# Fourteen unread products on TensorE during a weight load, and a further search of the order of work

## The chip, the cores and the metric

The kernel runs on one core of a Trainium2 chip. The metric is the time of one execution in microseconds of device time. Differences rest on several rounds, and I give them as ratios with a 95% interval. The record marks all runs told here as fast, with mean granted clocks of 0.987 to 0.995. The experiments were made on four chips, and the kernel before has a median of 1844.03 us on one and 1851.88 us on another, as far apart as the effects told here; so a ratio is always to before of the same rounds.

## The reference, cut to what matters

Four blocks one after the other, on 2048 tokens of width 512: a memory block A, a linear attention block B, A again, B again. B is short. A is a recurrence: 64 segments of 32 tokens, each attending to 8 memory rows that the segment before it wrote.

```python
for s in range(n_seg):                       # 64 segments of 32 tokens
    h = concatenate([mem, xs])               # 8 memory rows + 32 tokens
    q, k, v = h @ Wq, h @ Wk, h @ Wv         # 32 heads of 128
    p = softmax(mask(q @ k.T * scale))
    o = (p @ v) @ Wo
    mem = o[:8]                              # the next segment waits for this
    outs.append(o[8:])
```

## The kernel before

The kernel is built by a scheduler on the host. Every piece of work is a node with an engine, a cost and what it reads and writes; `schedule` plays them on a model of the engines, and the order that comes out is the fixed program of each engine. The rank of a node is its step times a period plus an offset from a table, and that table is what was searched.

```python
nd.prio = -(step * PERIOD + OFFSET[name][k])          # rank of a node
...
late.append(add("act", lambda a, W=W, v=v: a.dma_start(W[:, :, :], v), 0.5,
                writes=[nm], dsem="d" + nm, lat=t))   # Wq 13.2, Wk 23.7, Wv 34.8 us in the model
```

A projection is 16 products of 512 columns, four column tiles side by side. It is copied out of PSUM, the memory that TensorE's products are written to in this kernel (`pb` in the views), and turned (transposed), for half of the heads by a transposing DMA that the SP engine's queue issues, for the others by TensorE.

```python
QDMA = (True, False)                 # b = 0: by DMA, b = 1: by TensorE
def turned(W, key, blk, bkeys, b, dst, dkey, urgent, dma):
    tl = project(W, key, blk, bkeys, b, urgent)
    nd = evac(img[:, k, :], lambda: tl.f32()[:, :], 512, ...)
    if dma:
        add("sp", lambda e: e.dma_start_transpose(dst..., img[:, k, :]), 1.25, ..., lat=TURN)
        return nd
    ...                              # 16 transposes on TensorE and one copy
```

In the profile PE stands for TensorE's products, PEld for its weight loads, DVE for VectorE, ACT for ScalarE, POOL for GpSimd and SP for SyncE, which issues DMAs; a q after the name is the engine's sequencer, and "<-" names what ended a wait. The lines of the profile: L777 is the projection's product, L799 TensorE's turn, L790 the transposing DMA, L987 the output projection, L861 the memory scores, L1012 the next memory (the last product of a segment's recurrence), L608 and L609 the copies. In the changed kernel they are L789, L811, L802, L999, L873, L1024, L609 and L610, and L737 is the new product.

The softmax here doesn't subtract the row's maximum and nothing guards it: scores larger than these inputs give would overflow.

Of the kernel before, what the change touches and what calls it, by code (L numbers as in the profile page):

```python
# [16 lines left out]
HOP = 0.06  # L17
PE_SWITCH = 0.1
TURN = 1.8
MODE_SLACK = 12.41  # L20

LOOK = 0.074

PERIOD = 13.5
OFFSET = {
    "ld0": (3.45,),
    "ld1": (4.20,),
    "ld2": (-0.95,),
    "ld3": (-2.85,),
    "ld4": (0.40,),  # L30
    "startF": (12.05,),
    "prepF": (-11.05, 4.70, -9.25, -18.05, -7.00, -0.35, -15.95, -12.35, -15.40, 1.00, -1.65),
    "left0F": (-15.70, 1.30, -14.50, 0.25, -0.65, -12.60, 1.65, 6.55),
    "left1F": (15.35, 7.60, -6.60, 4.95, -3.45, 3.20, -0.65, 3.10),
    "leftv0F": (-1.70, -10.10),
    "leftv1F": (9.60, 0.00),
    "leftsF": (3.55, 9.85, 9.35, 1.25),
    "xlF": (1.05,),
    "qk0F": (0.15, 4.00, 2.75, -11.15, 1.55, 1.85, 11.40, 4.05),
    "qk1F": (0.00, -3.50, -2.10, -1.25, -25.90, -0.00, -5.45, 1.95),  # L40
    "v0F": (10.40, 1.50),
    "v1F": (31.95, 7.50),
    "mem0F": (2.55, 0.25, 5.85, -8.30, -1.20, -6.05, 2.15, 3.05, -1.60),
    "mem1F": (17.30, 12.60, 0.00, 1.10, -1.45, -6.00, -2.05, -21.65, 0.45),
    "outF": (1.85, -6.05, -5.85, -2.60),
    "nextF": (-0.45, -5.40, 13.70),
    "xF": (8.05, 1.50, -5.55, 5.05, -0.25, 9.95, 19.65, 5.95, -2.30, 7.20, 8.70, -12.05, -8.75, 4.00, -1.15,
        37.05, 0.30, 2.95, 10.30, 7.45, -2.10, 1.40, 0.10),
    "qk0": (-14.10, 1.50, -0.25, -5.35, -0.10, -0.05),
    "qk1": (1.55, 4.60, -0.05, -0.60, 1.80, 0.00, 7.10, -0.45),  # L50
    "v0": (0.35, -0.20),
    "v1": (5.15, 3.10),
    "mem0": (-5.20, -2.15, -1.60, -49.45, -13.55, -22.95, -3.35, -7.90, 4.70),
    "mem1": (7.10, -4.05, 3.25, -3.75, -2.90, 12.50, 5.15, -16.25, -12.15),
    "out": (-0.75, 4.95, 2.15, 0.00),
    "next": (1.75, 2.45, -4.05),
    "res": (48.90, 6.30, 2.30, -15.10, -1.45, -7.60, -2.50),
    "x": (2.45, 5.90, -2.85, -0.45, 6.20, 0.00, 15.70, -4.55, -22.30, 6.10, -15.10, 5.80, -2.55, 10.75, 6.10,
        0.60, 3.80, 21.60, 10.55, 5.20, 22.60, 29.30, 0.00),
    "prep": (7.35, -10.90, 1.30, 0.30, 10.40, -17.80, -4.90, 5.95, -3.00, -10.50, 9.70),  # L60
    "left0": (-4.00, -0.25, 18.45, -8.00, 1.40, -0.65),
    "left1": (0.10, 3.65, 0.45, 20.95, 3.05, -3.60),
    "leftv0": (32.60, 0.10),
    "leftv1": (11.30, 2.45),
    "lefts": (-2.95, 4.00, 0.50, -7.85),
    "xl": (6.35,),
    "bi": (0.25, -5.75, -1.85, -4.15, 6.60, -10.30, 9.70, -1.75, -6.35, 0.00, -15.35, 2.10, 7.40, -0.60, 21.85,
        -3.30, -3.50, 3.75, 0.00, 7.95, 2.05, 2.85, 12.85),
    "qk0L": (-9.45, 1.80, -2.10, 2.25, -3.65, 4.55, -0.30, 0.30),
    "qk1L": (-2.85, -6.75, -3.35, 4.40, -6.30, 2.10, -0.10, -1.70),  # L70
    "xL": (-6.30, -9.90, -7.95, -2.90, -3.60, 0.00, 4.70, 0.70, -2.85, 14.90, -19.10, 0.15, -0.20, 1.10, 6.60,
        0.15, -2.50, -0.30, -0.90, 0.00, -4.35),
    "lr": (-0.80, 7.55, 8.15, -13.30, 0.15, 7.95),
    "outL": (15.55, 3.95, 0.40, 10.10),
    "resL": (1.40, 4.60),
    "biL": (4.55, -5.70, -1.45, -34.70, -5.20, 0.75, 5.85, -1.90, -1.35, 0.15, 2.50, -24.50, -0.65, -21.55,
        1.05, 0.00, 0.00, 5.40, -1.60, -1.10, 11.15, -3.20, 3.85),
    "bm": (-3.95, -5.05, 16.55, 0.70, -0.20, 3.70, -9.00, 16.45, 0.15, -8.55, 2.25, 4.05, 2.75),
    "boF": (0.00, 7.10, -11.80, 3.35, 0.85, 0.75, -24.50, -13.85),
    "bo": (-1.10, 6.15, -2.70, -2.90, 0.00, -11.50, 1.10, -9.70),  # L80
    "ldL": (22.20, 1.70),
    "boL": (-26.60, 4.05, -1.85, -7.50, -5.65, -6.10, -13.50),
    "boZ": (18.15, -34.85, -14.20, 0.00, 8.30, -5.35, -7.10),
}


# [12 lines left out]
def c_pe(n_mm, n):  # L99
    return n_mm * max(0.0255, (n / 2.4 + 3.0) * 1e-3)  # L100
# [24 lines left out]
class _Prog:  # L125
# [80 lines left out]
    def schedule(self):  # L206
# [92 lines left out]
        def pick_for(e):  # L299
# [7 lines left out]
            while ready[e]:  # L307
# [17 lines left out]
                if pick is None:  # L325
# [3 lines left out]
                    held = item  # L329
                elif nd.prio < pick.prio - MODE_SLACK:  # L330
                    kept.append(item)
# [159 lines left out]
def _build_kernel(nc, A_x, A_mem0, A_Wq, A_Wk, A_Wv, A_Wo, A_seg_len, B_wqkv, B_wo, out):  # L491
# [26 lines left out]
    def sb(name, shape, dt=BF16):  # L518
        return E(nc.sbuf_tensor(name, shape, dt))

    Wq_sb = sb("Wq_sb", [128, 4, H * DH])
# [4 lines left out]
    x_sb = sb("x_sb", [128, NX, D])  # L526
    id_sb = sb("id_sb", [128, 128])
# [74 lines left out]
    P = _Prog(nc, banks)  # L602
    add = P.add
# [13 lines left out]
    x_view = A_x[0].rearrange("(t p) d -> t p d", p=128)  # L617
# [2 lines left out]
    o_view = out[0].rearrange("(t p) d -> t p d", p=128)  # L620
    qk_view = [W.rearrange("(c p) h e -> p c (h e)", p=128) for W in (A_Wq, A_Wk, A_Wv)]

    def x_move(o, i, k, reads, writes, kind, eng="pool"):
        add(eng, lambda e: e.dma_start(o, i), 1.1 if eng == "pool" else 0.4, reads=reads, writes=writes,
            dsem="%s%d" % (kind, k), lat=2.0)

    shift = [0]

    def slot(t):

        return (t + shift[0]) % NX
# [1 line left out]
    P.at(-9000, "ld0")  # L633
    add("sp", lambda s: s.dma_start(mem0_sb[0:M, :], A_mem0[0]), 0.1, writes=[MEM0], dsem="dmem", lat=2.0)
    P.at(-8000, "ld1")
    add("sp", lambda s: s.dma_start(x_sb[:, 0, :], x_view[0]), 0.4, writes=[("x", 0)], dsem="dx0", lat=2.0)
    late = []
    for i, (W, v, nm, t) in enumerate(((Wq_sb, qk_view[0], "Wq", 13.2), (Wk_sb, qk_view[1], "Wk", 23.7),
                                       (Wv_sb, qk_view[2], "Wv", 34.8))):
# [4 lines left out]
    for i in range(4):  # L644
        hs = slice(8 * i, 8 * i + 8)
        add("sp", lambda s, hs=hs: s.dma_start(Wo_sb[:, hs, :], wo_view[:, hs, :]), 0.9, writes=[("Wo", i)],
                 dsem="dWo%d" % i, after=[late[1 + i // 2]], lat=(12.5, 14.5, 7.3, 9.8)[i])
    add("sp", lambda s: s.dma_start(wqkv_sb[:, :, :], B_wqkv.rearrange("(c p) f -> p c f", p=128)), 0.5,
        writes=["wqkv"], dsem="dwqkv", after=[P.nodes[-1]], lat=5.0)
# [38 lines left out]
    for j in range(4):  # L688
        q = slice(32 * j, 32 * j + 32)
        d = j % 2  # L690
# [3 lines left out]
        o = 16 + 224 * d + 96  # L694
        sel(scr_sb[q, o:o + 24], ALU.not_equal, 1.0, -8, [[-1, 24]], 1, *SCR)

        o = 720 + 128 * d
# [3 lines left out]
        for g4 in range(4):  # L701
            o = 464 + 128 * d + 32 * g4 + 24
# [3 lines left out]
        writes=["selx"])  # L706
    add("dve", lambda v: v.tensor_copy(sell_sb[:, :, :].rearrange("p d c -> p (d c)"), scr_sb[:, 464:720]), 0.4, reads=SCR,
        writes=["sell"])
    add("dve", lambda v: v.tensor_copy(selz_sb[:, :, :].rearrange("p d c -> p (d c)"), scr_sb[:, 720:976]), 0.4, reads=SCR,
        writes=["selx"])  # L710
# [4 lines left out]
    tl = P.tile()  # L715
    add("pe", lambda t, tl=tl: t.matmul(tl.f32()[:, 0:128], A8_sb[0:8, :], A8_sb[0:8, :], start=True, stop=True), 0.06,
        reads=XV, tiles=[tl])
    evac(maskbd_sb[:, :], lambda tl=tl: tl.f32()[:, 0:128], 128, tiles=[tl], writes=["maskbd"])
    tl = P.tile()

    def _m0(t, tl=tl):
        for c in range(4):
# [2 lines left out]
    add("pe", _m0, 0.2, reads=[MEM0, "id"], tiles=[tl])  # L725
    evac(memT0_sb[:, :, :], lambda tl=tl: tl.bf16()[:, 0:4 * M].rearrange("p (c m) -> p c m", m=M), 32, tiles=[tl],
         writes=["memT0"])


    ln_no = [0]  # L730
# [31 lines left out]
    def a_layer(base, first):  # L762
        def at(s, name):

            P.at(base + s, name + ("F" if s <= 0 else "L" if s >= NSEG or (s == NSEG - 1 and name in LATE) else ""))
# [233 lines left out]
        def out_block(s):  # L999
            at(s, "out")  # L1000
            keys = [[("oTm", s % NO, b), ("oTx", s % NO, b)] for b in range(2)]
            return out_proj(oTb[:, s % NO, :, :], keys, True)
# [49 lines left out]
        if first:  # L1052
# [7 lines left out]
                writes=[(k, r, b) for k in ("oTx", "oTm") for r in range(NO) for b in range(2)])  # L1060
            add("dve", lambda v: v.memset(Pbx[:, :, :, :].rearrange("p h j q -> p (h j q)").bitcast(F32), 0.0), 0.8,
                writes=[("Pbx", j) for j in range(4)])

        def tokens(t, s):

            if not first:
                b_out(base + s, t, 0)
            elif t:
                at(s, "xl")
                x_move(x_sb[:, slot(t), :], x_view[t], slot(t), [], [("x", slot(t))], "dxl")  # L1070

        at(-4, "start")
        evac(hT[:, 0, 0, :, 0:8], memT0_sb[:, :, :], 32, reads=["memT0"], writes=[("hTm", 0, 0)])
# [3 lines left out]
        for s in range(NSEG):  # L1077
            G, g = divmod(s, 4)
            r2 = s % 2
            blk = hT[:, G % 2, g, :, :]  # L1080
            bk = [("hTm", G % 2, g), ("hTx", G % 2, g)]
            if g == 0 and G + 1 < NT:
                tokens(G + 1, s)
            for b in range(2):
                at(s, "qk%d" % b)
                hs = slice(4 * b, 4 * b + 4)
                turned(Wq_sb, "Wq", blk, bk, b, qT[:, r2, hs, :, :], ("qT", r2, b), True, QDMA[b] and 0 < s < NSEG - 1)
                turned(Wk_sb, "Wk", blk, bk, b, kT[:, r2, hs, :, :], ("kT", r2, b), True, KDMA[b] and 0 < s < NSEG - 1)
            for b in range(2):
                at(s, "v%d" % b)  # L1090
                tl = project(Wv_sb, "Wv", blk, bk, b, True)
                evac(vimg[:, r2, 512 * b:512 * b + 512], lambda tl=tl: tl.f32()[:, :], 512, tiles=[tl],
                     writes=[("v", r2, b)], urgent=True)
            if s + 1 < NSEG:
                for b in range(2):
                    mem_attention(s, b)
            w_of[s] = out_block(s)
            if s + 1 < NSEG:
                next_mem(s, w_of[s])
            if s > 0:  # L1100
                residual((s - 1) // 4, (s - 1) % 4, w_of[s])
                if g == 0:
                    b_in(base + s + 2, G - 1, not first)
            x_attention(s)
            if g == 2 and G + 1 < NT:
                prepare(G + 1, s)
            if s == NSEG - 1:
                at(s, "lr")
                add("pool", lambda p: p.memset(oTl[:, :, 24:32], 0.0), 0.5, writes=[("oTl", b) for b in range(2)])
                left_rows(NT - 1)  # L1110
# [206 lines left out]
```

## Time and profile before

| | before |
|---|---|
| median of the first three runs | 1848.17 us (1845.84 to 1848.36) |
| profiled execution | span 1843.1 us, mean granted clock 0.989 |
| TensorE busy | 1758.4 us, 95% |
| start, up to the end of segment 0's recurrence | 53.8 us |
| segments 3 to 62 of the first A block | 789.3 us |
| segments 63 to 125 of the second A block | 846.8 us |

The last three rows are from the trace: the start of the sixteenth and last L1012 product of each segment. I count segments from 0 to 62 in the first block and from 63 to 125 in the second (the last segment of a block hands no memory on and has no such product). (Some expectations below count ordinally: their tenth segment is 9.) The prediction below shows the page and views of this profile. One more line of the page is needed later, the queue (packets, MB, share of 16 engines' time) that brings instructions:

```profile
q8 instruction: 365, 5.98, 1.3%
```

TensorE's own instructions would explain it: 46,693 products and as many weight loads, 93,386 instructions, over 365 packets are 256 a packet, and 5.98 MB over 365 are 16.4 KB a packet. I call 256 such instructions, or their packet, a block.

### The profile page before, as it was taken

What the parts mean: (1) busy time and instruction counts of PE and PEld (TensorE: products, weight loads), DVE (VectorE), ACT (ScalarE), POOL (GpSimd) and SP (SyncE); (2) the same over time, 40 slices, a digit from 0 to 9 for tenths busy, and PEclk for the clock granted to TensorE, in tenths of its full rate; (3) what the DMA queues carried; (4) which work ended last, traced back from release to release, by engine and by line L of the source; (5) the groups of instructions that cost most, each with busy time, mean ns of one, the idle gap of its engine ahead of it and who ended that gap; (6) DMA issues with size and microseconds to landing.
All of it is one profiled execution on the core that took longest, in us unless ns stands there. A gap on an engine that the chain in (4) does not pass through costs nothing.

```text
span 1843.1 us, 100858 instructions
## 1 busy us (share of the span) xinstructions
PE 1758.4 (95%) x46693; PEld 1194.1 (65%) x46693; DVE 1017.6 (55%) x3168; ACT 1207.6 (66%) x3127; POOL 76.9 (4%) x182
## 2 busy tenths in 40 slices
PE   5899999999999999999799999999999999999997
PEld 2566676666666767666566666666666666666663
DVE  2355555555555555555545555566555556555566
ACT  3566666766666666666466667666667666666665
POOL 3000000000000000000000000000000000000000
PEclk8999999999999999999899999999999999999999
DMA  9312122212221221211012122122122222122223
GB/s 366 85 37 42 38 44 35 47 38 44 38 41 41 35 46 38 44 37 38 22 29 39 37 41 46 39 42 43 38 41 46 41 43 41 41 43 41 52 62 99
DMA packets 218934, 94.85 MB, mean 51 GB/s; under 512 B 202536, under 2 KB 212656, under 8 KB 216976
## 3 DMA queue, kind: packets, MB, share of 16 engines
q1 hardware_dynamic: 211312, 60.22, 17.7%
q0 software_dynamic: 5616, 15.60, 2.9%
q10 hardware_dynamic: 1584, 12.58, 1.7%
q8 instruction: 365, 5.98, 1.3%
q14 instruction: 57, 0.47, 0.1%
HBM read 29.63 MB, written 10.49 MB: 22 GB/s over the span
## 4 chain that ended last, share of the span: by engine, by line
PE 83%; DMA 11%; ACT 3%; DVE 2%; issue 1%; ACTq 0%; DVEq 0%
PE pb L777 38%; PE pb L987 16%; DMA arena_sb<-arena_sb 9%; PE pb L959 3%; PE pb L861 3%; PE pb L1029 3%; PE pb L799 3%; PE pb L1137 3%; PE pb L916 2%; ACT arena_sb L608 2%; PE pb L878 2%; PE pb L1173 1%; DMA Wk_sb<-in_A_Wk_dram 1%; PE pb L892 1%; PE pb L891 1%
## 5 line engine op out<-in xcount | busy, mean ns | idle before, releaser
L608 ACT ACTIVATE arena_sb<-pb 128x512 bf16<-128x512 f32 (+6 forms) x1412 | 727.2, 523 | 359.8 <-PE pb L777 302.1
L777 PE MATMUL pb<-Wq_sb,arena_sb 128*32 128x512 bf16 x5120 | 357.5, 383 | 0.6 <-DMA Wq_sb<-in_A_Wq_dram 0.6
L777 PE MATMUL pb<-Wv_sb,arena_sb 128*32 128x512 bf16 x5120 | 356.9, 382 | 0.1
L777 PE MATMUL pb<-Wk_sb,arena_sb 128*32 128x512 bf16 x5120 | 343.5, 381 | 6.6 <-DMA Wk_sb<-in_A_Wk_dram 5.2
L987 PE MATMUL pb<-Wo_sb,arena_sb 128*32 128x256 bf16 x10368 | 326.4, 273 | 5.8 <-issue 3.7
L987 PEld LDWEIGHTS pb<-Wo_sb,arena_sb 128*32 128x32 bf16 x10368 | 261.5, 96 | 34.8 <-DVE arena_sb L895 13.8
L944 DVE TENSOR_TENSOR arena_sb<-arena_sb 32x256 bf16<-32x256 bf16 x512 | 213.3, 417 | 119.8 <-ACT arena_sb L940 108.7
L609 DVE CAST arena_sb<-pb 128x128 bf16<-128x128 f32 (+3 forms) x334 | 118.5, 355 | 252.5 <-PE pb L1012 201.4
L609 DVE COPY arena_sb<-pb 128x512 bf16<-128x512 bf16 (+2 forms) x352 | 137.7, 392 | 204.5 <-PE pb L799 198.9
L777 PEld LDWEIGHTS pb<-Wk_sb,arena_sb 128*32 128x32 bf16 x5120 | 141.8, 97 | 126.1 <-DMA Wk_sb<-in_A_Wk_dram 5.3
L777 PEld LDWEIGHTS pb<-Wq_sb,arena_sb 128*32 128x32 bf16 x5120 | 133.4, 97 | 113.6 <-DVE arena_sb L609 24.2
L777 PEld LDWEIGHTS pb<-Wv_sb,arena_sb 128*32 128x32 bf16 x5120 | 134.4, 98 | 86.3 <-issue 4.4
L608 ACT ACTIVATE outW_sb<-pb 128x128 fp32r<-128x128 f32 x261 | 72.3, 277 | 114.4 <-PE pb L987 77.1
L799 PEld LDWEIGHTS pb<-id_sb,arena_sb 128*32 128x32 bf16 x4352 | 77.5, 97 | 90.8 <-ACT arena_sb L608 58.1
L959 PE MATMUL pb<-arena_sb 128*128 128x128 bf16 x1024 | 130.9, 217 | 0.0
L799 PE MATMUL pb<-id_sb,arena_sb 128*32 128x128 bf16 x4352 | 109.6, 221 | 14.7 <-ACT arena_sb L608 14.6
L946 DVE TENSOR_TENSOR arena_sb<-arena_sb 32x64 bf16<-32x64 bf16 x512 | 111.1, 217 | 15.8
L960 PE MATMUL pb<-arena_sb 128*128 128x32 bf16 x1024 | 118.3, 177 | 0.0
L868 ACT ACTIVATE arena_sb<-pb 128x256 bf16<-128x256 f32 x252 | 96.1, 383 | 27.3 <-PE pb L861 20.6
L861 PE MATMUL pb<-arena_sb 128*128 128x32 bf16 x2016 | 97.0, 178 | 5.2 <-DMA arena_sb<-arena_sb 4.9
L895 DVE TENSOR_TENSOR arena_sb<-pb,arena_sb 128x128 bf16<-128x128 f32 x252 | 72.2, 286 | 42.0 <-ACT arena_sb L883 27.6
L861 PEld LDWEIGHTS pb<-arena_sb 128*128 128x128 bf16 x2016 | 74.6, 96 | 30.0 <-DMA arena_sb<-arena_sb 6.4
(121 smaller groups left out, 2304.5 us busy)
## 6 DMA issues: line engine op xcount, KB each, us to landing
arena_sb<-arena_sb SPq DMA_TRANSPOSE x368, 2.5
Wq_sb<-in_A_Wq_dram ACTq DMA_DIRECT2D x1, 4096.0 KB, 13.6
Wk_sb<-in_A_Wk_dram ACTq DMA_DIRECT2D x1, 4096.0 KB, 24.3
Wv_sb<-in_A_Wv_dram ACTq DMA_DIRECT2D x1, 4096.0 KB, 34.6
Wo_sb<-in_A_Wo_dram SPq DMA_DIRECT2D x4, 1024.0 KB, 11.6
xs_scratch<-x_sb POOLq DMA_DIRECT2D x32, 128.0 KB, 2.1
pq_scratch<-arena_sb POOLq DMA_DIRECT2D x32, 128.0 KB, 2.8
x_sb<-xs_scratch POOLq DMA_DIRECT2D x16, 128.0 KB, 2.3
```

Of the source, the lines that this page charges most:

```text
L608: return e.activation(o() if callable(o) else o, i() if callable(i) else i, ACTF.Copy)
L609: return e.tensor_copy(o() if callable(o) else o, i() if callable(i) else i)
L777: r = pe.matmul(tl.f32()[32 * j:32 * j + 32, 0:512], blk[:, c, :], W[:, c, o:o + 512], start=(c == 0), stop=(c == 3), tile_position=(0, 32 ...
L799: r = pe.transpose(tt.bf16()[32 * j:32 * j + 32, 128 * i:128 * i + 128], img[:, k, o:o + 32], id_sb[:, :], tile_position=(0, 32 * j))
L861: r = pe.matmul(tl.f32()[:, o:o + 32], kk[:, hh, :, :].rearrange("p j x -> p (j x)"), qT[:, r2, hh, :, 0:8], start=True, stop=True)
L868: add("act", lambda a: a.activation(Pm[:, k, :, :].rearrange("p a q -> p (a q)"), tl.f32()[:, 0:256], ACTF.Exp, scale=SCALE), c_act(256), ...
L895: add("dve", lambda v: v.tensor_tensor(oTb[:, s % NO, 16 * b:16 * b + 16, 0:8], pv.f32()[:, 0:128].rearrange("p (n q) -> p n q", q=8), Rm[ ...
L944: add("dve", lambda v, q=q, j=j: v.tensor_tensor(Pbx[q, :, j, 0:32], Px[q, :, :], Rx[q, :, :], ALU.mult), c_dve(256) + 0.075, reads=["Px", ...
L946: add("dve", lambda v, q=q, j=j: v.tensor_tensor(Pbx[q, :, j, 32:40], PLL[q, g2, :, gl], Rx[q, :, 0:8], ALU.mult), c_dve(64) + 0.075, read ...
L959: pe.matmul(o, vimg[:, r2, e], Pbx[:, hh, :, 0:32], start=True, stop=False)
L960: return pe.matmul(o[:, :, 0:8], vleft[:, g2, e], Pbx[:, hh, :, 32:40], start=False, stop=True)
L987: r = pe.matmul(tl.f32()[32 * j:32 * j + 32, 0:256], oT[:, 4 * hh + n, :], Wo_sb[:, 8 * n + hh, 256 * d:256 * d + 256], start=(hh == 0 and ...
```

## The change

Two intents. TensorE runs fourteen products into a bank that nobody reads, meant, as I take it, to keep its clock at 1.00 where before has it at 0.70 (38 to 39 us) and 0.50 (39 to 45 us). And the table of offsets is searched further, after two token loads were given their real latency in the model. The diff, cut to its core:

```diff
-MODE_SLACK = 12.41
+MODE_SLACK = 11.85
 OFFSET = {
-    "ld0": (3.45,),
+    "ld0": (13.20,),
     ... nearly every other offset changes as well ...
+    "warm": (2000.00,),
 }
...
-    add("sp", ... x_view[0]), 0.4, writes=[("x", 0)], dsem="dx0", lat=2.0)
+    add("sp", ... x_view[0]), 0.4, writes=[("x", 0)], dsem="dx0", lat=8.5)
...
+    def warm(step, n, after):
+        P.at(step, "warm")
+        tl = P.tile()
+        for i in range(n):
+            if i:
+                P.again()
+            add("pe", lambda pe: pe.matmul(tl.f32()[0:32, 0:512], id_sb[:, 0:32], Wq_sb[:, 0, 0:512],
+                                           start=True, stop=True, tile_position=(0, 0)),
+                c_pe(1, 512), reads=["id", "Wq"], tiles=[tl], mode="col", after=after if i == 0 else ())
...
+            if first and s == 0:
+                warm(0, 14, [n for n in P.nodes if n.key == (0, "mem1F", 1)])
```

The token load of the second group gets the same 8.5 us.

## The prediction

> **What bounds the kernel now.** I read the page first: engine shares, then the slices with the granted clock, then the chain that ended last.
>
> ```profile
> PE 1758.4 (95%) x46693; PEld 1194.1 (65%) x46693; DVE 1017.6 (55%) x3168; ACT 1207.6 (66%) x3127; POOL 76.9 (4%) x182
> ...
> PE   5899999999999999999799999999999999999997
> ...
> PEclk8999999999999999999899999999999999999999
> ...
> PE 83%; DMA 11%; ACT 3%; DVE 2%; issue 1%; ACTq 0%; DVEq 0%
> ```
>
> TensorE is busy for 1758.4 of 1843.1 us, so only 84.7 us of the span show it idle, and 83% of the chain is TensorE's own work. Three places are weak: the first two slices (46 us each), the slice in the middle, where one layer ends and the next starts, and the last one. Second view: engine busy time in chosen stretches. The columns are the stretch, its length, the busy time of PE, PEld, DVE, ACT and POOL with instruction counts, the granted clock, the DMA share and GB/s.
>
> ```profile
> 25.60:31.60 6.00, 5.99 (x84) 2.76 (x88) 0.42 (x1) 1.39 (x3) 0.00 (x0) 0.50 1.03 425
> 36.70:39.50 2.80, 0.96 (x41) 0.58 (x45) 0.99 (x4) 1.06 (x4) 0.00 (x0) 0.80 1.10 348
> 39.50:45.10 5.60, 5.60 (x60) 2.07 (x52) 2.94 (x10) 2.18 (x5) 0.00 (x0) 0.50 1.19 264
> 59.90:63.00 3.10, 0.05 (x4) 0.06 (x8) 0.00 (x0) 0.70 (x2) 0.78 (x1) 0.88 0.99 139
> 75.00:870.00 795.00, 777.78 (x21345) 539.12 (x21341) 438.55 (x1393) 541.14 (x1441) 24.39 (x45) 1.00 0.21 40
> 923.00:1771.00 848.00, 831.13 (x22426) 568.42 (x22418) 484.88 (x1537) 572.56 (x1466) 31.11 (x57) 1.00 0.22 41
> ```
>
> The two long rows are the recurrent segments of the two layers: idle 795.00 - 777.78 = 17.2 us and 848.00 - 831.13 = 16.9 us, all at clock 1.00. The other rows are the start. TensorE works at clock 0.50 for about 6 us after the key weights land, and for 5.6 us again with the value weights[...]. Third view: TensorE's timeline there, which says what the idle time was.
>
> ```profile
> 36.67 0.29 PE L916 MATMUL pb<-arena_sb 128*32 128x32 bf16 x18
> 38.19 0.27 PE L916 MATMUL pb<-arena_sb 128*32 128x32 bf16 x14 [1.23 <-issue]
> 38.39 0.28 PE L716 MATMUL pb<-arena_sb 8*128 8x128 bf16 x1
> 39.28 0.41 PE L935 MATMUL pb<-arena_sb,bo_sb 128*32 128x256 bf16 x4 [0.61 <-DVE arena_sb L922]
> 39.48 0.27 PE L932 MATMUL pb<-arena_sb,bo_sb 128*32 128x64 bf16 x4
> 39.55 5.32 PE L777 MATMUL pb<-Wv_sb,arena_sb 128*32 128x512 bf16 x48
> ```
>
> The value products (L777 with Wv) were queued behind the first segment's token scores (L916) and their sums (L935), and the score group was itself cut in two by 1.23 us in which no releaser shows. The list of DMA issues says when the value weights came:
>
> ```profile
> Wv_sb<-in_A_Wv_dram ACTq DMA_DIRECT2D x1, 4096.0 KB, 34.6
> ```
>
> Its issue starts at 1.83 us in the timeline, so they had landed at 1.83 + 34.6 = 36.4 us. The 3.1 us from there to 39.55 is therefore not a wait for that transfer; this is the first thing the change's title leads a reader to misjudge.
>
> [...] clock 0.50 after the pauses before the key weights (5.15 us) and before 62.95 us (3.05 us). Between them, from 36.96 to 39.28, the short groups at 38.19 and 38.39 did not save it: the one-microsecond rows have it at 0.70 from 38 to 39 and at 0.50 after that. [...] Here four column tiles run side by side: 48 value products are 12 rounds, the chain gives them 5.12 us cold, 427 ns a round; 88 warm ones (22 rounds) in the steady state take 4.76 us, 216 ns a round. [...] The page of before has an instruction queue with 365 packets and 5.98 MB, 16.4 KB each[...]. That the 1.23 us cut inside one run of equal products was a late block, at a time when the DMA share is 1.1, is my reading; the trace shows only that no semaphore ended it.
>
> **The change, part by part.**
>
> (a) It adds fourteen products of 512 columns into a spare PSUM bank. They use only the first column tile, so they don't run four abreast: 14 x 216 ns = 3.02 us if warm, 14 x 427 = 5.98 us if cold. Nothing evacuates them, but their tile holds a bank until the next owner takes it. They are ordered after the second memory-score block of the first segment (its L861 products, last group near 36 us in the kernel before) and have the lowest rank of all work, so the host-side scheduler puts them where its own model finds TensorE with nothing else ready. That model knows no cold clock: it loses no time on the 6 us at half speed from 25.6, so it believes TensorE is some 3 us ahead of where it is, with a gap of about 3 us before 36.4. On the chip that gap doesn't stand before 36.4, but after it.
>
> (b) What they buy. If they run from about 36.3, warm (the clock row is 1.00 from 31.7 to 38.3), they end near 39.3: they take the place of the 2.8 us in which TensorE did 0.96 us of work, and the value products start about where they did, 39.3 to 40.3. What changes is their speed: 12 rounds at 216 instead of 427 ns save 12 x 0.211 = 2.53 us; the sums and key products of the rest of the cold stretch (up to 45.15) save about 0.3 more. Gain 2.8 us, less up to 0.8 us for scores and sums that may now come after the fourteen: 2.0 to 2.8. I take 2.5.
>
> (c) Does it reach the end? After 45 us TensorE works without a gap to 59.9, then waits 3.05 us on ACT, which waits on transposes by DMA behind the load of the other block's weights (1536 KB, issued at 53.19 from a queue in order). Earlier evacuations let that queue come to this load earlier, so the wait moves along with the work; the output weights are there at 47.5, when the DMA share drops, and are first used at 51.1, so 2.5 us earlier still finds them. I carry 80%: 2.0 us.
>
> (d) The token loads' model latency goes from 2.0 to 8.5 us for the first two. The measured one is 8.5 us, so the order of the first 15 us now fits the chip, but TensorE waits there for the query weights (14.4 us) anyway: 0 us by itself.
>
> (e) The search: nearly every offset changes, and the slack for staying in a tile mode from 12.41 to 11.85. No arithmetic is added or removed; the same 46,693 products run, plus fourteen. What can be won is bounded by idle time: 34.1 us in the two steady stretches, of which these rows are the largest:
>
> ```profile
> PE pb L799 <- ACT arena_sb L608: 5.3, 10, 1.0
> PE pb L861 <- DMA arena_sb<-arena_sb: 3.9, 6, 1.1
> PE pb L827 <- DMA arena_sb<-arena_sb: 3.2, 5, 0.8
> ...
> PE pb L827 <- DMA arena_sb<-arena_sb: 8.4, 10, 1.4
> PE pb L799 <- ACT arena_sb L608: 4.4, 9, 1.0
> ```
>
> They are the waits of the first layer, then of the second: 25.2 us of stalls under 1.5 us each, the kind that an order removes. Besides, switches between column tiles and whole-array products hide in busy time: the timeline of one segment shows steps of about 0.1 us (406.95 to 407.28, where 0.22 is used), several in each of 128 segments, so 40 to 60 us by estimate, though an already searched order keeps most. I give the search a tenth of 34 + 50 = 84, which is 8 us in its own model, and about 70% of that on the chip: 5.5 us. This is a judgement, not a reading.
>
> (f) Middle (900 to 920: 10.55 us busy of 20) and end (1795 to 1843) are chains of dependent single steps, DVE and ACT in turn; an order shortens them little. One cut of 1.81 us and one of 1.91 us with no releaser stand in the end, at 1797.69 and 1804.45, and may move or stay: +-1 us, mean -1.
>
> Sum: -2.0 + 0 - 5.5 - 1.0 = -8.5 us, from 1848.2 to about 1839.5 us.
>
> **The rivals.** First: the fourteen cost what they buy. If TensorE reaches them late, or they run cold, they delay value weights that have been there since 36.4 us by 3 to 6 us and the gain of (b) is cancelled[...]. For it: the landing at 36.4. Against: the idle time stood there anyway, and the author kept the change. This makes the start 0 to +3 us and the total 1842 to 1845. Second: the gain is made at 40 us and lost at 60, because the wait for the transposes keeps its absolute time with the transfers it stands behind. For it: the DMA share is about 1.0 from 57 to 60. Against: that load starts when its queue gets there, not at a fixed time. Total about 1842. Third: the search finds much more than a tenth, 15 us or more, if it removes the transposes' waits (16.5 of the 25.2 us) and switches as well. For it: nearly all offsets moved. Against: the kernel is already searched, and its busy tenths are all 9. Total about 1830. Fourth: the search fits its model, not the chip; the steady part is unchanged or 3 us worse, total 1846 to 1850.
>
> **Range and chances.** The three runs of before spread over 2.5 us, so noise is about +-1.5 us. Mean 1839.5; the start can give 0 to -4 and the search +2 to -15, which adds up to a range of 1828 to 1847. Faster by over 2% means below 1811.2 us, 37 us off, more than all the steady idle time: 2%. Slower by over 2% means above 1885, which only a broken order could do: 1%. Within 2%: 97%.
>
> **What would show each step.** (a), (b): a row of fourteen products reading Wq into a bank in TensorE's timeline near 36 to 40 us, 216 ns apart, the one-microsecond clock rows at 1.00 through 38 to 46 instead of 0.50, and the value products at 216 ns a round. (c): the pause now at 59.9 to 63.0 comes 2 us or more earlier and is no longer. (e): the idle time of the two steady stretches below 34 us, and the distance from the first segment's value products to the last segment's, in each layer, shorter. If instead the clock is still 0.50 after the fourteen, (b) is wrong; if the steady stretches lose 10 us or more, I have sized the search too small; if they gain, it fits its model alone.

## The result, and the profile after

Ratios here are the mean time of one kernel's fast runs over that of the other's of the same rounds, so they are not quite the ratio of the medians that stand beside them.

| | before | changed |
|---|---|---|
| median of 4 runs | 1847.01 us (1845.42 to 1848.36) | 1845.42 us (1844.32 to 1849.27) |
| ratio | 1 | 0.9995, 95% interval 0.9977 to 1.0014 |
| profiled execution | 1843.1 us | 1847.5 us, the slowest of its four |

The time lies in the range, but the forecast change of 8.5 us is not there. The page of the changed kernel, busy shares, granted clock and chain:

```profile
PE 1758.5 (95%) x46707; PEld 1174.2 (64%) x46707; DVE 1027.4 (56%) x3172; ACT 1205.9 (65%) x3123; POOL 76.9 (4%) x182
...
PEclk9999999999999999999899999999999999999998
...
PE 82%; DMA 12%; ACT 2%; DVE 2%; issue 1%; ACTq 0%; DVEq 0%
```

The first digit of the clock row went from 8 to 9: the start is warmer. And the DMA share of the chain went up from 11 to 12%. The stretches of the prediction, in the changed kernel:

```profile
36.70:39.50 2.80, 1.20 (x21) 0.60 (x22) 1.44 (x6) 0.38 (x1) 0.00 (x0) 1.00 1.09 349
39.50:45.10 5.60, 5.60 (x78) 2.33 (x80) 3.11 (x10) 3.11 (x8) 0.00 (x0) 1.00 1.18 269
59.90:63.00 3.10, 2.31 (x58) 1.42 (x56) 1.12 (x5) 1.53 (x5) 0.00 (x0) 1.00 0.31 111
75.00:870.00 795.00, 772.71 (x21163) 524.35 (x21160) 436.63 (x1381) 537.62 (x1429) 24.38 (x45) 1.00 0.21 40
923.00:1771.00 848.00, 829.25 (x22355) 555.83 (x22348) 489.91 (x1531) 568.30 (x1457) 31.11 (x57) 1.00 0.22 41
```

The clock is 1.00 where it was 0.50 (39.5 to 45.1) and the pause at 60 us is nearly gone. The two long rows show more idle time than before, 41.0 us together against 34.1. Their counts are 182 and 71 products short of before's: the trace has all 46,707 products, but the work stands shifted against these windows (124 more products before 75 us, 92 more after 1771 us). So I use the distances between segments instead. The new products in TensorE's timeline:

```profile
36.15 0.38 PE L737 MATMUL pb<-Wq_sb,id_sb 128*32 128x512 bf16 x1
36.16 0.49 PE L928 MATMUL pb<-arena_sb 128*32 128x32 bf16 x17
38.30 0.27 PE L928 MATMUL pb<-arena_sb 128*32 128x32 bf16 x15 [1.65 <-issue]
38.40 1.67 PE L737 MATMUL pb<-Wq_sb,id_sb 128*32 128x512 bf16 x7
...
40.16 0.39 PE L737 MATMUL pb<-Wq_sb,id_sb 128*32 128x512 bf16 x1
...
40.52 0.81 PE L737 MATMUL pb<-Wq_sb,id_sb 128*32 128x512 bf16 x3
40.96 0.40 PE L789 MATMUL pb<-Wv_sb,arena_sb 128*32 128x512 bf16 x3
41.17 0.38 PE L737 MATMUL pb<-Wq_sb,id_sb 128*32 128x512 bf16 x1
```

They are warm (seven in 1.67 us), but only one runs before the cut, which is now 1.65 us, and the value products start at 40.96 instead of 39.55 us. The pause at 60 us, with the issue of the weight load before it (first before, then the changed kernel):

```profile
53.19 1.52 SPq L648 DMA_DIRECT2D arena_sb<-in_B_wqkv_dram  x1
62.95 0.62 PE L799 MATMUL pb<-id_sb,arena_sb 128*32 128x128 bf16 x16 [3.05 <-ACT arena_sb L608]
```

```profile
48.98 0.58 SPq L649 DMA_DIRECT2D arena_sb<-in_B_wqkv_dram  x1
60.74 0.27 PE L873 MATMUL pb<-arena_sb 128*128 128x32 bf16 x4 [0.80 <-DMA arena_sb<-arena_sb]
```

SP reaches the 1536 KB load after one transpose instead of two, 4.2 us earlier, and the transposes behind it come earlier too. So the changed kernel is ahead: segment 3 ends at 90.54 us instead of 94.87, a lead of 4.3 us. By segment 16 the lead is gone (267.19 against 267.14), at segment 62 the changed kernel is 2.0 us behind, at segment 125 3.9 us. Up to segment 16 the lead is lost in single segments: 5 (0.8 us), 15 (1.7) and 16 (1.0); what segment 8 gains (1.1) segment 9 gives back (1.2), and all others are within 0.3 us. Of the 121 segments from 5 on, 63 take the same time in both kernels to 0.15 us.

### The profile page after: what moved, and what is told of

The parts are those of the page before. It is cut to its first block, busy times and chain, and to the rows that moved or that the text cites. A ratio compares the mean times of both kernels' runs of the same rounds, so it can differ in the third digit from the quotient of the medians.

```text
span 1847.5 us, 100872 instructions
## 1 busy us (share of the span) xinstructions
PE 1758.5 (95%) x46707; PEld 1174.2 (64%) x46707; DVE 1027.4 (56%) x3172; ACT 1205.9 (65%) x3123; POOL 76.9 (4%) x182
## 4 chain that ended last, share of the span: by engine, by line
PE 82%; DMA 12%; ACT 2%; DVE 2%; issue 1%; ACTq 0%; DVEq 0%
PE pb L789 37%; PE pb L999 16%; DMA arena_sb<-arena_sb 11%; PE pb L873 3%; PE pb L971 3%; PE pb L1151 3%; PE pb L1041 3%; PE pb L811 3%; PE pb L928 2%; ACT arena_sb L609 2%; PE pb L890 2%; PE pb L1187 1%; DMA Wk_sb<-in_A_Wk_dram 1%; PE pb L904 1%; PE pb L903 1%
## 5 line engine op out<-in xcount | busy, mean ns | idle before, releaser
L609 ACT ACTIVATE arena_sb<-pb 128x512 bf16<-128x512 f32 (+4 forms) x1410 | 721.2, 519 | 332.8 <-PE pb L789 271.4
L789 PE MATMUL pb<-Wv_sb,arena_sb 128*32 128x512 bf16 x5120 | 352.9, 380 | 0.4 <-issue 0.2
L789 PE MATMUL pb<-Wq_sb,arena_sb 128*32 128x512 bf16 x5120 | 349.0, 383 | 0.9 <-DMA Wq_sb<-in_A_Wq_dram 0.6
L999 PEld LDWEIGHTS pb<-Wo_sb,arena_sb 128*32 128x32 bf16 x10368 | 255.5, 96 | 25.8 <-issue 7.9
L610 DVE COPY arena_sb<-pb 128x512 bf16<-128x512 bf16 (+1 forms) x334 | 134.1, 402 | 204.8 <-PE pb L811 196.7
L610 DVE CAST arena_sb<-pb 128x384 bf16<-128x384 f32 (+3 forms) x354 | 129.9, 368 | 210.1 <-PE pb L1024 157.5
L789 PEld LDWEIGHTS pb<-Wk_sb,arena_sb 128*32 128x32 bf16 x5120 | 135.7, 97 | 132.9 <-DMA Wk_sb<-in_A_Wk_dram 5.7
L789 PEld LDWEIGHTS pb<-Wq_sb,arena_sb 128*32 128x32 bf16 x5120 | 125.4, 97 | 125.9 <-DVE arena_sb L610 24.4
L789 PEld LDWEIGHTS pb<-Wv_sb,arena_sb 128*32 128x32 bf16 x5120 | 127.5, 97 | 89.6 <-issue 2.7
```

The source lines that it names most:

```text
L609: return e.activation(o() if callable(o) else o, i() if callable(i) else i, ACTF.Copy)
L610: return e.tensor_copy(o() if callable(o) else o, i() if callable(i) else i)
L789: r = pe.matmul(tl.f32()[32 * j:32 * j + 32, 0:512], blk[:, c, :], W[:, c, o:o + 512], start=(c == 0), stop=(c == 3), tile_position=(0, 32 ...
L999: r = pe.matmul(tl.f32()[32 * j:32 * j + 32, 0:256], oT[:, 4 * hh + n, :], Wo_sb[:, 8 * n + hh, 256 * d:256 * d + 256], start=(hh == 0 and ...
```

## The experiments

Fifteen runs, each timed in five rounds. All gave correct results.

### Which part of the change does what

Theory 1 said that the start is gained and kept and the new order costs; theory 2, that the lead is given back whatever the order; theory 3, that the order gains and the products cost. Four kernels on one chip. The first is before with the products alone:

```diff
+    def warm(...)        # as in the change
+            if first and s == 0:
+                warm(0, 14, ...)
```

> The kernel before with the fourteen products alone, old order (TensorE's order differs from before's in the first hundred or so groups alone). Theory 1, the start is gained and kept, the searched order costs: 3.0 to 4.5 us under before, and the fourth segment's memory products 3.5 to 4.5 us earlier than the 94.9 us of before. Theory 2, the head start is given back in later waits whatever the order: earlier by 3.5 to 4.5 us at the fourth segment too, but within 1 us of before at the end. Theory 3, the order gains and the products cost: slower than before by 1 us or more.

The second is the changed kernel without them:

```diff
-                warm(0, 14, [n for n in P.nodes if n.key == (0, "mem1F", 1)])
```

> The changed kernel without the fourteen products, new order. Theory 1: 2 to 4 us over before. Theory 2: within 1 us of before. Theory 3: 2 to 5 us under before.

The third takes before's start, no products, and the new offsets of all other segments:

```diff
 OFFSET = {
     ... names that end in F, and ld0 to ld4, as before ...
-    ... all others as before ...
+    ... all others as changed ...
```

> Old offsets for the first segments of each layer and no fourteen products, new offsets for all the rest (TensorE's order is that of before up to group 791, of the changed kernel in the second layer's body). Theory 1: 2 to 4 us over before, all of it after the fifth segment. Theory 2: within 1 us of before. Theory 3: 2 to 5 us under.

The fourth is the changed kernel again, without an edit:

> The changed kernel once more, for five rounds and a second trace. All theories: within 0.15% of before, as its first four runs had it (0.9995). If a second trace loses its time in other segments than the first (there: the tenth, sixteenth and seventeenth, forty-fourth), single late segments are chance; if in the same ones, they belong to the order.

| run | median us | ratio to before | 95% interval |
|---|---|---|---|
| warm_only | 1852.63 | 1.0033 | 1.0020 to 1.0046 |
| after_no_warm | 1844.84 | 0.9996 | 0.9975 to 1.0017 |
| steady_new | 1844.45 | 0.9987 | 0.9974 to 1.0001 |
| after_again | 1846.81 | 1.0001 | 0.9984 to 1.0017 |
| before, same rounds | 1845.78 | | |

Theories 1 and 2 both fall. The products alone make before slower by 0.33%, 6 us, although TensorE's program differs from before's only near them, within the first hundred or so groups; and the order alone does little. At segment 3 warm_only is 1.1 us ahead of before (93.8 against 94.9 us), not the 3.5 to 4.5 that theories 1 and 2 had asked for. Theory 3 has the sign, but no reason why fourteen products at 36 to 41 us should cost anything at segment 15. The trace of warm_only has its own late segments, and they are in part those of the changed kernel in the other order: 5, 15, 16, 43, 44.

So I measured it over all segments. For each trace: the time from one segment's last L1012 product to the next's, less the tenth percentile over all traces compared of the segments in the same place of a group of four of the same block (13.0, 13.5, 12.8 us and so on). This leaves how late each segment is; 115 segments (5 to 61, 67 to 124) are compared. The late times of the two changed-kernel traces correlate at 0.88, and with warm_only, in the *old* order, at 0.81 and 0.85; but with before, after_no_warm and steady_new only at 0.45 to 0.59. Those three, of two different orders, correlate among themselves at 0.83 to 0.88. Late segments do not follow the order of work. They follow whether the fourteen products are in the program.

### The place in the instruction stream

New theory, A: what counts is the place of TensorE's instructions in their 256-instruction blocks. Fourteen products with their weight loads are 28 instructions, and everything after them moves by 28 places. Rival B: the wide products cost by themselves. To move the program without wide products I put tiny ones at its very start, where TensorE waits for the first tokens:

```diff
+    def pad(n):
+        P.at(-7000, "pad")
+        tl = P.tile()
+        for i in range(n):
+            ...
+            add("pe", lambda pe: pe.matmul(tl.f32()[0:32, 0:8], id_sb[:, 0:32], id_sb[:, 0:8], ...), ...)
+    pad(14)              # before_pad14; 114 in warm_only_pad114 and after_pad114; 50 in after_pad50
```

In each of these the rest of TensorE's order is that of its parent. With 114, the fourteen wide ones and the tiny ones make 128, one whole block.

> The kernel before with fourteen tiny products (8 columns) at the very start, where TensorE idles anyway: they move every later TensorE instruction by 28 places, as the fourteen wide ones do[...]. Theory A, place: TensorE's instructions come in 16 KB blocks (256 instructions) by DMA, a block's packet delays a transpose that is in flight, and the shift by 28 decides which transposes are hit: 3 to 8 us over before, and the late segments are those of the kernels with the wide products (correlation of the excess per segment with them 0.75 or more, with before's 0.65 or less). Theory B, the wide products cost by themselves[...]: within 1 us of before, excess as before's.

> The fourteen wide products in the old order plus 114 tiny ones at the start: 128 products, 256 instructions, one whole block. Theory A: excess per segment like before's again (0.75 or more), time 1 to 3 us under before, so 7 to 9 us under the run without the 114. Theory B: still 5 to 7 us over before.

> The changed kernel plus the same 114 tiny products. Theory A: 1 to 4 us under before and under the changed kernel. Theory B: as the changed kernel, within 1 us of before.

> The changed kernel plus 50 tiny products: 64 products, 128 instructions, half a block. Theory A: a third set of late segments, correlated with neither of the other two above 0.7; its time can lie either side, from 6 us over to 6 us under before. Theory B: as the changed kernel, within 1 us of before.

And, after these, a control, a hybrid and two repeats on one chip. The control has 128 tiny products and nothing else (`pad(128)` in before). The hybrid has the new offsets for the names that end in F and before's for all others, with the wide products and `pad(114)`.

> Control: the kernel before plus 128 tiny products at the start, a whole block of 256 instructions, and no wide products. Theory A (the place in the block decides): within 0.1% of before, excess per segment correlated with before's at 0.75 or more, where fourteen tiny products cost 0.42%. If tiny products cost by their number, nine times as many cost more than 0.42%.

> New offsets for the first segments of each layer, the fourteen wide products, old offsets for the rest, and 114 tiny products, so that the block phase is before's. If the new order pays in the start, where it works together with the wide products: 3 to 5 us under before (0.9973 to 0.9984), as the changed kernel with the same 114 was. If it pays in the steady segments: within 1 us of before, as the old order with wide products and 114 was.

> The changed kernel with 114 tiny products once more, on the same chip as the changed kernel itself. Theory A: 0.15 to 0.35% under before, and 0.15% or more under the changed kernel. If its first result was luck: within 0.1% of both.

> The changed kernel again, for the comparison with the run before on one chip: within 0.15% of before, late segments those of its first two traces (correlation 0.8 or more).

| run | shift, instructions | median us | ratio to before | 95% interval |
|---|---|---|---|---|
| before_pad14 | 28 | 1855.39 | 1.0042 | 1.0022 to 1.0061 |
| warm_only_pad114 | 256 | 1850.53 | 1.0009 | 0.9992 to 1.0026 |
| after_pad114 | 256 | 1843.74 | 0.9975 | 0.9957 to 0.9992 |
| after_pad50 | 128 | 1852.28 | 1.0026 | 1.0005 to 1.0046 |
| before, same rounds | 0 | 1849.46 | | |
| before_pad128 | 256 | 1844.51 | 1.0007 | 0.9992 to 1.0022 |
| start_new_pad114 | 256 | 1847.47 | 1.0013 | 1.0001 to 1.0025 |
| after_pad114_again | 256 | 1840.41 | 0.9983 | 0.9968 to 0.9997 |
| after_third | 28 | 1846.73 | 1.0018 | 1.0006 to 1.0030 |
| before, same rounds | 0 | 1844.03 | | |

Theory A holds. Fourteen tiny products, which are over at 2.9 us, where TensorE idles, cost 0.42%, 7.8 us; 128 of them cost nothing that can be told from zero. The changed kernel with a whole block is 0.35% faster than the changed kernel on the same chip (0.9983 against 1.0018, intervals apart). Two expectations failed in size: warm_only_pad114 was to beat before and only equals it, so the wide products in the old order bring nothing that five rounds can see; and it is 0.24% (4.4 us) under warm_only, not 7 to 9 us, on another chip and with intervals that overlap. after_third was to be within 0.15% of before and is 0.18% over. The hybrid, at 1.0013, met neither of its two expectations, and its trace says that it was no fair test: it did not get the changed kernel's start. Its weight load stands behind two transposes again (issued at 51.95 us, against 47.58 in after_pad114), TensorE waits 4.17 us before 62.73, and segment 3 ends at 95.1 us, against 90.1 and 90.0 in the two runs of after_pad114.

Which segments are late, by place (the first block's segments that are over 0.8 us late in the trace of each run):

```
shift 0    before              25 31 47 59
shift 256  before_pad128       31 32 44 47 49 53 59
shift 256  after_pad114_again  25 31 44 47 49 59          (other order, wide products)
shift 28   before_pad14        5 15 21 31 43 44 49 59 60 61
shift 28   after               5 9 15 16 31 43 44 53 59 60 (other order)
shift 128  after_pad50         11 12 24 27 33 39 41
```

Over all traces up to here, and the 192-place one below, the late times of two kernels at the same place (0 and 256 counted as one) correlate at 0.78 to 0.89, 38 pairs of either order; those at different places at 0.24 to 0.65. (after_pad82's trace lacks 108 products of 46,789, none of them L1012's.) In time: from segment 3 to 62 and from 63 to 125 the eight traces at place 0 take 792.5 + 844.8 us on average, the five at 28 take 795.3 + 849.8, which is 7.8 us more. TensorE's largest waits from 75 to 870 us in before_pad14 (total us, times, longest) are those that the prediction shows of before (there 3.9, 5.3 and 3.2 us), and longer:

```profile
PE pb L877 <- DMA arena_sb<-arena_sb: 6.5, 10, 1.0
PE pb L815 <- ACT arena_sb L609: 6.3, 10, 1.3
PE pb L843 <- DMA arena_sb<-arena_sb: 3.9, 6, 0.9
```

### How a block makes a segment late

Theory A1: the packet of a block delays the transposes that are in flight. A2: late blocks stall TensorE. For A1 speaks the trace. Segment 15 is on time in before and late in before_pad14, whose order is the same. The DMA view of the stretch in which its query and key transposes are issued, before first, from 243.4 to 245.9 us (a queue's packets, MB and share; an issue's median us to landing):

```profile
q1 hardware_dynamic: 544, 0.13, 25.7%
...
arena_sb<-arena_sb SPq DMA_TRANSPOSE x2, 2.4
```

The same of before_pad14, from 240.6 to 244.6 us, with the chain and with TensorE's wait:

```profile
q8 instruction: 1, 0.02, 1.5%
...
arena_sb<-arena_sb SPq DMA_TRANSPOSE x2, 3.5
```

```profile
240.65 3.94 DMA arena_sb<-arena_sb
...
244.67 0.61 ACT arena_sb L609
...
245.32 0.41 PE pb L815 x16
```

```profile
245.32 0.41 PE L815 MATMUL pb<-id_sb,arena_sb 128*32 128x128 bf16 x16 [0.79 <-ACT arena_sb L609]
```

In before the blocks around this segment come at 241.16 and 247.24 us, either side of the transposes (243.46 to 247.17), which take 2.41 and 2.47 us. In before_pad14 a block comes at 242.54, in the midst of them, and they take 3.94 and 3.14. ACT's next copy, in its fixed order, waits for the first of them, and TensorE's turn waits for that copy: the page's "PE waits for ACT" is a wait for a transpose. The whole trace of before shows the same. Of its transposes that are not behind another one, the 29 that no block's packet meets take 2.42 us, nine in ten of them 2.43 or less; the 120 that meet one take 3.31 us on average, one in ten over 4.2. (A longer one meets a packet more easily; but what is alone has next to no spread, 2.51 at most.) A block's packet takes 1.08 us on average. There are 365 blocks and 368 transposes, about three each in a segment. Not every block does harm: only those, as I read it, that hit a transpose that the recurrence waits for.

For A2 speaks the cut of 1.23 us in before. It stands after TensorE's 350th product in before, warm_only, steady_new, after_no_warm and all three traces of the changed kernel, and in after_pad50, after the 351st in before_pad14, and after the 478th, 350 + 128, in the five kernels with 128 added, whatever the products are. (after_pad82 shows no such cut.) In all these traces TensorE goes on 1.2 to 1.5 us after the end of a block's packet (in before 38.19 us, the packet having ended at 36.88). So I take these cuts for late blocks, 1.0 to 1.8 us each, while the weights load. To tell how much of the shift's cost is this, I took all DMA transposes out:

```diff
-    QDMA = (True, False)
-    KDMA = (True, False)
+    QDMA = (False, False)
+    KDMA = (False, False)
...
-                turned(Wq_sb, ..., False, step > 0)      # the left rows; the same for Wk
+                turned(Wq_sb, ..., False, False)
```

> The kernel before with every turn of query and key images made by TensorE instead of by a DMA transpose (a base for the next run; the offsets of the added steps are guesses). All theories: slower than before, by 2 to 8%, since TensorE takes on some 370 turns of about 0.23 us and their evacuations, and no transpose is left in the DMA list.

> The same without DMA transposes, plus the fourteen tiny products at the start, 28 places. Theory A1 (a block's packet delays transposes in flight): with no transposes the shift costs nothing, within 0.1% of the run before. Theory A2 (late blocks stall TensorE itself): the shift still costs 0.2 to 0.5%, as it did with transposes (0.42%).

And a fourth place for the changed kernel, `pad(82)`:

> The changed kernel plus 82 tiny products: 96 products, 192 instructions, three quarters of a block. Theory A1: a fourth set of late segments, correlated below 0.7 with the three known ones; the time lies anywhere from 0.4% under to 0.4% over before, and its late time in the segments goes with it. If the place in the block did not matter: as the changed kernel with 114 tiny products, 0.15 to 0.25% under before.

| run | median us | ratio to before | 95% interval |
|---|---|---|---|
| pe_turn | 1928.71 | 1.0419 | 1.0405 to 1.0434 |
| pe_turn14 | 1931.08 | 1.0432 | 1.0418 to 1.0446 |
| after_pad82 (shift 192) | 1842.11 | 0.9957 | 0.9944 to 0.9971 |
| before, same rounds | 1851.88 | | |

Without DMA transposes the shift costs 0.13% in place of 0.42%, and the intervals of the pair overlap, so it is not told from zero; I had said within 0.1%. The traces are plainer. In the first block no segment of either kernel is late any more: the late time of segments 5 to 61 sums to 0.3 and 0.1 us, measured against these two kernels' own tenth percentiles, where it is 15 to 24 us with DMA transposes. (In the second block 11.9 and 12.8 us are left, nearly all in every fourth segment from 71 on, in both alike; with transposes it is 22 to 33.) Segments 3 to 62 and 63 to 125 together take 1722.8 and 1723.5 us, 0.7 us apart, where the two places are 7.8 apart with transposes. TensorE's waits from 75 to 870 us, pe_turn, then pe_turn14 (total us, times, longest):

```profile
PE pb L987 <- DVE arena_sb L895: 11.1, 15, 0.8
PE pb L750 <- DVE arena_sb L744: 3.0, 13, 0.3
```

```profile
PE pb L1003 <- DVE arena_sb L911: 11.1, 15, 0.8
PE pb L766 <- DVE arena_sb L760: 2.9, 13, 0.2
```

These two are the same to 0.1 us; pe_turn14 has two more of 0.2 us with no releaser. A1 is the way in the segments; A2 is, by the cuts as I read them, at work at the start, where they stay (1.31 us after the 350th product of pe_turn), and whether it has a part in the remaining 0.13% these runs do not tell. Turning by TensorE is no remedy: it costs 4.2%.

The fourth place has a fourth set of late segments (7, 8, 9, 29, 35, 36, 51, 52, 53) and is, by its ratio, the fastest kernel, 0.43% under before, just past the 0.4% that I had allowed; the changed kernel's three ratios, 0.9995, 1.0001 and 1.0018, all have intervals above it. It was run in one set of rounds only, and not beside the changed kernel. Its trace does not say why it is so fast: its segments take 1638.8 us (3 to 62 and 63 to 125), where the new order at place 0 takes 1636.1, so the expectation that the time goes with the late time of the segments is not borne out. That stays open.

## Why the prediction was right or wrong

*The reading of the start* held. The value weights were no wait, the clock is 1.00 through the stretch, the fourteen are warm. The cut was in all likelihood a late block, as I had read it: it stands at the 350th product or one whole block later, and a block's packet ends 1.2 to 1.5 us before its end.

*(a) and (b), 2.5 us at the value products*: the clock was 1.00 as forecast, the size was not. That the products would hold the clock was my estimate. I had all fourteen run before the value products at 39.3 to 40.3; they started at 40.96, as my first rival feared, and the 48 end only 0.2 us earlier than in before (44.69 against 44.86). I had also taken before's trace for typical, where all 48 ran cold, each over 0.6 us long against 0.38 warm; in after_no_warm, steady_new and before_pad14 it was 24, 28 and 28, and in before_pad128, pe_turn and pe_turn14, also without wide products, none. In the ten traces with the wide products none of the 48 is that slow; but in after_pad50 the clock is 0.50 from 36.49 to 39.91 us and the first of the fourteen themselves run cold. So these runs do not show that the products hold the clock.

*(c), 2.0 us carried*: the lead came, from another place. Segment 3 ends at 90.5, 91.0 and 89.6 us in the changed kernel, and at 94.9, 94.2, 92.1 and 92.4 in the four traces with the old start and no wide products: 3.0 us on average instead of 2.0, because the pause at 60 us shrank when a weight load went ahead of a transpose. One trace of the new offsets without wide products has 92.5, and there the load is behind two transposes again, as it is in warm_only and in the hybrid (95.1 us): only the programs with both all the new offsets and the products have it behind one. One reading of the prediction was wrong here: the last of the output weights lands at 49.25 us in before, not 47.5.

*(d), 0 us*: not tested by a run. (In a build with the products and the new latency but the old offsets I found TensorE's order to be that of warm_only; no run shows it.)

*(e), 5.5 us for the search*: this term was too large. At place 0 the old order's four traces take 1638.6 us for segments 3 to 62 and 63 to 125 together, the new order's four 1636.1; at place 28 it is 1645.9 (two) and 1644.7 (three). So the search is worth 1 to 2.5 us in the segments; the timed steady_new says 0.13%, 2.4 us, with an interval that reaches 1. My evidence was the waits on transposes, which I took for the kind that an order removes. For a large part they weren't: they are hits by instruction blocks, and the segments in which they stand change with the place. (Of the 25.2 us the transposes' rows that the prediction shows are 15.5; its 16.5 takes in a row of 1.0 that isn't among them.)

*(f), -1 us*: nothing; the end after segment 125 is 57.0 us before and 57.5 in the changed trace.

*The step that failed* is in (e): "No arithmetic is added or removed; the same 46,693 products run, plus fourteen." I counted the fourteen only where they run, although I had the page's 365 packets of 16.4 KB before me. They also move the 46,000 products behind them by 28 places, and that costs 0.42% in before and, for the changed kernel, 0.35% where it was compared on one chip. Without this term my sum would have been off by half, not in sign: with the place put back the change is worth 0.25 and 0.17%, 4.6 and 3.1 us, not 8.5. With it, gain and cost cancel. None of my rivals was this one; the second, "made at 40 us and lost at 60", had the shape, not the place. The sum of the parts (-3.0 start, -1 to -2.5 order, +6.5 to +7.8 place) comes out at +1.0 to +3.8, against the measured -0.9 to +3.3; one trace of the changed kernel differs from the next by up to 3.9 us in the segments. And the range was added up wrongly: the worst ends of its parts, +2 for the search and 0 for the start and the end, reach 1850, not 1847.

## What to carry to other kernels

In this long unrolled program 28 added instructions at the start cost 0.42% (1.0022 to 1.0061) and 256 none that can be told from zero (1.0007, 0.9992 to 1.0022); before's transposes take 3.31 us on average where a block's packet meets them, against 2.42. So, in a program of this kind, test an edit against a control that pads the program by as many dummy instructions, before believing that it or a searched order helped or hurt; and try a few paddings: those of the changed kernel lie between 0.9957 and 1.0026 of before, the change itself between 0.9995 and 1.0018. Where a lead from a local gain vanishes in a handful of segments, compare which segments are late across kernels before asking why.
